# State reads of seven batches with four heads side by side in the TensorE array, transposed by DMA, beside M's session

## The chip, the cores and the metric

The kernel runs on one core of one Trainium2 chip. The metric is the device time of one execution in microseconds; before it is 205.8 us, the median of three runs (205.37 to 205.98). Engines are named as in the profile: PE (TensorE, matrix products into the accumulator memory PSUM), DVE (VectorE), ACT (ScalarE), POOL (GpSimd) and SP (SyncE, which here issues most DMAs). Each engine works through its own instructions in order and meets the others at semaphores.

## What is computed

Cross attention in both directions between 512 rows x and 32 state rows, for 8 batches and 8 heads of 64 columns; then the rows of all heads, side by side, go through a two-layer network with a leaky ReLU.

```
B, H, S, Ns, D = 8, 8, 512, 32, 64          # batches, heads, rows of x, rows of state, columns
a      = softmax(scale * x @ state.T)        # over the state rows
xread  = a @ state
a2     = softmax(scale * state @ x.T)        # over the rows of x
sread  = a2 @ x                              # the read of the states: 32 x 64 for each batch and head
x      = concat([xread, sread], axis=rows)   # heads side by side: (8 * 544) x 512
h      = x @ w_in                            # 512 x 2048
out    = max(0.01 * h, h) @ w_out            # 2048 x 512
```

The change touches `sread = a2 @ x` alone, and the form in which its result is kept.

## The kernel before

The rows that come from x (512 a batch) and those that come from the states (32 a batch) go different ways. For the rows of x the product `xread @ w_in` is not formed from xread: for each batch the kernel computes M = state @ w_in by heads (`a_m`, L326) and then the first layer as a @ M (`ff1`, L347, 16 blocks of 128 output columns each, two matmuls of 512 columns to a block, followed by the leaky ReLU on ACT at L352). The second layer (`Fast.unit`, L532) multiplies in seven products instead of eight on 2 x 2 blocks, with the sums of operands on DVE (L521) and of results on DVE and POOL (L544, L602).

The rows of the states wait until the end. Each batch's read is kept, transposed, in one tile `sr_t` (L141): the 128 partitions are the columns of two neighbouring heads, and the free sizes are 4 pairs of heads and the 256 state rows of all batches. After the last batch, `FastIn` (L365 and on) puts all 256 rows through the first layer, again in seven products: `x_sums` (L398) forms sums of blocks of `sr_t` on DVE, `product` (L416) multiplies weights by blocks of `sr_t` or of those sums.

The order is written by hand: what each engine does comes in the order of the source. The main part is a loop over batches 2 to 7 with 16 steps `s` each. A step has one `ff1` of this batch and some units of the second layer of the batch before (`fill`); between them stand, at fixed steps, the pieces of the next batch's attention: in step 1 its scores (L205) and the last quarter of this batch's M, in steps 5 to 11 its two softmaxes, and behind step 10 the first three quarters of its M. That last group, three blocks of 8 matmuls (24 in all), is called M's session here. The projections of M and the scores run with the array divided in pieces of 64 rows and 32 columns (64*32 in the profile); `ff1` and the second layer use the whole array (128*128).

The read of a state (`a_sread`, L295 to L309) needs `a2T`, the transposed probabilities of the second softmax, which a DMA on SP's queue makes from `a2` (L291); a batch's `a2T` has two buffers. For each pair of heads k it runs 4 matmuls of 64 columns, one for each 128 rows of x; the weights are the 128 columns of both heads of x, the moving operand is the 2 x 32 columns of `a2T` of both heads. Of the four products of two heads by two heads only the two of equal heads are wanted: two ACT casts (L306) take them from PSUM to `sr_t`, 64 partitions each. Batches 0, 1 and 2 are read in steps 4, 6 and 8 of batch 2, and each later batch in its own step 8. The bank is that of tag "big".

PSUM has the tags "ph" (two banks, used in turn by `ff1` and the third block of M's session, which takes both), "py" (two), "big" and "sc" (two banks each as one). A matmul that opens a bank waits until its last reader is done.

On SP's queue stand, in order, loads of x (L99), the transposes of `a2` (L291) and of x (L189), the state loads (L169) with their transposes (L176), and the stores of results (L478, L569). An instruction that waits there holds up those behind it.

Of the kernel before, what the change touches and what calls it, by code (L numbers as in the profile page):

```python
# [9 lines left out]
P = 128  # L10
B, H, S, D = 8, 8, 512, 64
NS = 32
# [3 lines left out]
NT = S // P  # L16
NK = H // 2
SCALE = 1.0 / (D ** 0.5)

BF16 = mybir.dt.bfloat16  # L20
FP32 = mybir.dt.float32
# [6 lines left out]
def kernel(  # L28
# [9 lines left out]
    nc = tc.nc  # L38

    consts = ctx.enter_context(tc.tile_pool(name="consts", bufs=1))  # L40
# [15 lines left out]

    st0f = consts.tile([P, 4, D], FP32, name="st0f")
    nc.scalar.dma_start(  # L60
        st0f[:], state[0:2].rearrange("b h n d -> (b h n) d").rearrange("(p r) d -> p r d", r=4)
    )
# [75 lines left out]
    st1 = consts.tile([P, P], BF16, name="st1")  # L138
    groups = ((2, 4), (4, 8))
    st_t = [consts.tile([P, hi - lo, P], BF16, name=f"st_t{lo}") for lo, hi in groups]  # L140
    sr_t = consts.tile([P, NK, B * NS], BF16, name="sr_t")  # L141

    stb0 = consts.tile([P, 4, D], BF16, name="stb0")

# [14 lines left out]
            ps[:, :, D:].rearrange("p r (k q) -> p k q r", q=8),  # L159
        )  # L160

    stf = [consts.tile([P, hi - lo, P], FP32, name=f"stf{lo}") for lo, hi in groups]
    stb = [consts.tile([P, hi - lo, P], BF16, name=f"stb{lo}") for lo, hi in groups]

    def load_state(i):
# [129 lines left out]
    def a_sread(a):  # L295
        ps = psum.tile([P, NK, 2, NS], FP32, name="psr", tag="big", bufs=1)
        for k in range(NK):
            for i in range(NT):
                nc.tensor.matmul(  # L299
                    ps[:, k, :, :],  # L300
                    lhsT=a.xb[:, i, 2 * k:2 * k + 2, :].rearrange("p h d -> p (h d)"),
                    rhs=a.a2T[:, :, i, NS * k:NS * (k + 1)],
                    start=(i == 0), stop=(i == NT - 1),
                )
        for g in range(2):
            nc.scalar.copy(  # L306
                sr_t[D * g:D * (g + 1), :, NS * a.b:NS * (a.b + 1)],
                ps[D * g:D * (g + 1), :, g, :],
            )  # L309

# [21 lines left out]
    def m_evict(a, c, pm, copy):  # L334
        cols = slice(DM * c, DM * (c + 1))
        if isinstance(pm, list):
            for g in range(2):
                copy(a.M[:, g, cols], pm[g][:])
        else:
            copy(a.M[:, :, cols], pm[:])  # L340
# [24 lines left out]
    class FastIn:  # L365
# [4 lines left out]
        def __init__(self, hT):  # L370
            w = w_in_bf[:].rearrange("p (r k) (i f) -> p i r k f", r=2, i=2)
            self.W = {(i, r): w[:, i - 1, r - 1] for i in (1, 2) for r in (1, 2)}
            x = sr_t[:].rearrange("p (r k) (c t) -> p r c k t", r=2, c=2)
            self.X = {(r, c): x[:, r - 1, c - 1] for r in (1, 2) for c in (1, 2)}
            self.hT, self.S, self.T = hT, {}, {}
            self.bank, self.sv = [{}, {}], [None, None]
# [11 lines left out]
        def x_sums(self):  # L388
            X, T = self.X, self.T
            t = att.tile([P, 4, 2, P], BF16, name="tx", tag="aT")  # L390
            for n in (0, 2, 1, 3):
                u, v, op = (
                    (X[1, 2], X[1, 1], ALU.subtract), (X[1, 1], T.get(2), ALU.subtract),
                    (X[2, 2], X[1, 2], ALU.add), (T.get(1), X[2, 1], ALU.add),
                )[n]
                T[n] = t[:, n]
                with nc.allow_low_precision(reason="operands of a product"):
                    nc.vector.tensor_tensor(out=T[n], in0=u, in1=v, op=op)  # L398

        def product(self, r, n):  # L400
            b = self.bank[r]
            if n in (1, 2):
                tag = ("ph", "ph") if r == 0 else ("big", "sc")
                b[n] = psum.tile([P, self.R, P], FP32, name="pf", tag=tag[n - 1], bufs=2 - r)[:]
            bank = b[n] = b[{1: 1, 6: 1, 7: 1, 4: 1, 2: 2, 5: 2, 3: 2}[n]]
            W, X = self.W, self.X
            lhs = {1: W[1, 1], 2: W[1, 2], 4: W[2, 2]}.get(n)
            if lhs is None:
                lhs = self.S[{3: 3, 5: 0, 6: 1, 7: 2}[n]]
            rhs = {1: X[1, 1], 2: X[2, 1], 3: X[2, 2]}.get(n)  # L410
            if rhs is None:
                rhs = self.T[{4: 3, 5: 0, 6: 1, 7: 2}[n]]
            for q in range(self.R):
                j = self.R * r + q
                for k in range(2):
                    nc.tensor.matmul(  # L416
                        bank[:, q, :], lhsT=lhs[:, k, P * j:P * (j + 1)], rhs=rhs[:, k, :],
                        start=(n in (1, 2, 5) and q == 0 and k == 0), stop=(k == 1),
                        skip_group_check=True,
                    )  # L420
            self.done(r, n, bank)
# [480 lines left out]
    for b in range(2, B):  # L902
        hT = hpool.tile([P, 16, S], BF16, name="hT", tag="hT")
        a = att_of[b]
        nxt = att_of[b + 1] if b + 1 < B else None
        now = Batch(b, hT)
        std = []
        if b == 2:
            std = [(i, 3) for i in range(2)] + [(i, jq) for i in range(2, NT) for jq in range(4)]

        def fill(s):
            n = (PACE2 if b == 2 else PACE)[s]
            left = min(n, len(before.units)) if before else 0
            if left:
                before.run(left)
            if n > left:
                now.run(n - left)

        for s in range(16):
            if s == 11:  # L920
                fill(s)
            ff1(a, hT, s)
            if s == 0:
                if b + 2 < B:
                    load_x(b + 2, nc.sync)
                    open_xb(b + 2)
                a_a2t(a)
                if before:
                    for n in (0, 1):
                        before.f.sums(n, 4, 8)  # L930
            elif s == 1:
                if nxt is not None:
                    a_scores(nxt)
                m_evict(a, 3, a_m(a, 3, "big"), SCA)
                if nxt is not None:
                    a_shift(nxt)
                if b + 2 < B:
                    for h in range(0, H, 2):
                        cast_x(b + 2, h, h + 2, POO)
                if before:  # L940
                    before.f.sums(2, 4, 8)
            elif s == 3:
                if before:
                    before.f.sums(3)
                if nxt is not None:
                    a_max2(nxt)
                if b == 2:
                    weights_sum(0)
                    weights_sum(2)
            elif s == 4:  # L950
                if b == 2:
                    load_state(1)
                    a_sread(a0)
            elif s == 6:
                if b == 2:
                    a_sread(a1)
            elif s == 8:
                a_sread(a)
                if b == 2:
                    state_t(1)  # L960
                    weights_sum(1)
                    weights_sum(3)
            elif s == 12:
                for n in range(3):
                    now.f.sums(n, 0, 4)
            if nxt is None:
                if s == 4:
                    fi = FastIn(None)
                    for n in range(3):
                        fi.w_sum(n)  # L970
                elif s == 10:
                    fi.w_sum(3)
                    fi.x_sums()
            if s == (11 if b == 2 else 7) and b + 2 < B:
                a_open(att_of[b + 2], b + 2)
                a_xt_dma(att_of[b + 2])
            if nxt is not None:
                if s == 5:
                    a_exp(nxt)
                elif s in (7, 8):  # L980
                    a_exp2(nxt, s - 7)
                    if s == 7:
                        a_probs(nxt)
                elif s == 11:
                    a_probs2(nxt)
                elif s in (12, 13):
                    SCA(nxt.M[:, s - 12, DM:2 * DM], pm1[:, s - 12, :])
            if std:
                i, jq = std.pop(0)
                piece(1, h1, i, jq)  # L990
            elif s != 11:
                fill(s)
            if s == 10 and nxt is not None:
                pm0 = a_m(nxt, 0, "big")
                pm1 = a_m(nxt, 1, "sc")
                pm2 = a_m(nxt, 2, "ph")
                for g, copy in enumerate((VEC, SCA)):
                    copy(nxt.M[:, g, 2 * DM:3 * DM], pm2[g][:])
                m_evict(nxt, 0, pm0, SCA)
        before = now  # L1000
# [90 lines left out]
```

## Time and profile before

| | |
|---|---|
| three runs, us | 205.98, 205.37, 205.80 |
| profiled execution, us | 205.83 |
| its span in the profile, us | 204.1 |
| mean granted TensorE clock | 0.997 |
| HBM read / written, MB | 17.30 / 8.91 |

How to read it: times are microseconds from the start of the span unless marked ns. "PE" are matmuls, "PEld" the loads of their weights. Matmuls overlap, and their ends are modelled, so what a matmul costs is read from the distance between the starts of two. A group row names engine, line, operation, output <- inputs, then for PE the part of the array (rows*columns) and the shape (partitions x elements); "xN" is the number of instructions. The chain of waits is followed back from the last instruction to what released each step, and lists pieces with start, length and name. "SPq" is SP's queue, whose rows give the time that the issue of a DMA took.

### The profile page before, as it was taken

To read this page: it belongs to the slowest core of one execution; us is meant where nothing else is said; L and a number is where in the kernel's file an instruction comes from. 1 tells how busy PE (TensorE), PEld (TensorE's weight loads), DVE (VectorE), ACT (ScalarE), POOL (GpSimd) and SP (SyncE) were. 2 spreads that over 40 slices of the span, in tenths; PEclk is the share of its full clock that TensorE was granted. 3 is DMA by queue.
4 is the path that set the end of the run, shared out by engine and by line. 5 is a ranking of instruction groups with operands and counts; after the bars stand their busy time and mean duration, and the time that the engine had idled before them with its cause. 6 is when DMAs were issued, how large, how long until landed. Compare 5 with 4: busy or idle time off the path is not lost.

```text
span 204.1 us, 4531 instructions
## 1 busy us (share of the span) xinstructions
PE 197.5 (97%) x1852; PEld 126.4 (62%) x1852; DVE 152.6 (75%) x231; ACT 145.0 (71%) x272; POOL 40.5 (20%) x66
## 2 busy tenths in 40 slices
PE   7889999999999999999999999999999999999992
PEld 2443534434345557766776767676767677799882
DVE  1767689688999869976996699669968853685622
ACT  3458748579859796978797878788778856467710
POOL 8831002004005104400402040200020002004250
PEclk9999999999999999999999999999999999999998
DMA  6999994889576596939452755250016000410035
GB/s 176 230 207 272 231 248 135 133 273 227 113 230 172 144 171 179 95 114 290 83 95 106 229 131 108 102 157 5 0 53 207 0 3 26 180 55 3 0 90 167
DMA packets 38772, 27.74 MB, mean 136 GB/s; under 512 B 24352, under 2 KB 35744, under 8 KB 38752
## 3 DMA queue, kind: packets, MB, share of 16 engines
q1 hardware_dynamic: 33552, 20.65, 39.6%
q0 software_dynamic: 4912, 6.55, 15.7%
q10 hardware_dynamic: 288, 0.26, 0.6%
q8 instruction: 14, 0.23, 0.4%
q14 instruction: 6, 0.05, 0.1%
HBM read 17.30 MB, written 8.91 MB: 128 GB/s over the span
## 4 chain that ended last, share of the span: by engine, by line
PE 77%; DMA 15%; SPq 2%; POOL 2%; DVE 1%; issue 1%; ACT 1%; POOLq 0%; ACTq 0%
PE yq L532 36%; PE ph L347 22%; DMA x<-in_x_dram 7%; PE py L462 6%; DMA stf<-in_state_dram 3%; PE pf L416 3%; PE yu L532 3%; PE pm L326 3%; DMA xf<-in_x_dram 3%; DMA xT<-xb 2%; PE psr L299 2%; SPq L169 1%; PE sc L205 1%; PE phw L358 1%; ACT M L340 1%
## 5 line engine op out<-in xcount | busy, mean ns | idle before, releaser
L352 ACT ACTIVATE hT<-ph 128x512 bf16<-128x512 f32 x108 | 63.4, 603 | 22.3 <-PE ph L347 21.7
L347 PE MATMUL ph<-aT,M 128*128 128x512 bf16 x216 | 62.3, 379 | 0.0
L532 PEld LDWEIGHTS <-su 128*128 128x128 bf16 x416 | 39.4, 98 | 13.6 <-DVE su L521 1.7
L532 PEld LDWEIGHTS <-hT 128*128 128x128 bf16 x288 | 27.7, 98 | 12.8 <-issue 2.1
L532 PE MATMUL yq<-tw_xf,su 128*128 128x256 bf16 x192 | 27.2, 273 | 0.0
L532 PE MATMUL yq<-w_out_bf,hT 128*128 128x256 bf16 x192 | 27.0, 273 | 0.0
L347 PEld LDWEIGHTS <-M 128*128 128x128 bf16 x216 | 21.0, 98 | 9.4 <-DVE aT L247 0.5
L105 POOL CAST xb<-xl 128x512 bf16<-128x512 f32 (+1 forms) x21 | 14.8, 746 | 57.0 <-DMA xl<-in_x_dram 57.0
L521 DVE TENSOR_TENSOR su<-hT 128x1024 bf16<-128x1024 bf16 x24 | 16.7, 697 | 10.5 <-ACT hT L352 10.5
L462 PE MATMUL py<-w_out_bf,hT 128*128 128x512 bf16 x96 | 24.2, 379 | 0.0
L462 PEld LDWEIGHTS <-hT 128*128 128x128 bf16 x128 | 11.8, 98 | 14.3 <-issue 1.5
L602 POOL TENSOR_TENSOR yo<-sv,sv 128x512 f32<-128x512 f32 x6 | 7.8, 1303 | 57.4 <-ACT sv L541 41.5
L544 DVE TENSOR_TENSOR yo<-yq,sv 128x512 f32<-128x512 f32 x17 | 11.6, 685 | 6.5 <-PE yq L532 6.5
L541 ACT COPY sv<-yq 128x512 f32<-128x512 f32 x24 | 13.9, 585 | 2.0 <-PE yq L532 1.4
L340 ACT CAST M<-pm 128x1024 bf16<-128x1024 f32 x13 | 13.2, 1014 | 0.7 <-PE pm L326 0.6
L532 PE MATMUL yq<-w_out_bf,su 128*128 128x256 bf16 x96 | 13.1, 273 | 0.0
L532 PE MATMUL yq<-tw_x,su 128*128 128x256 bf16 x96 | 13.1, 272 | 0.0
L532 PE MATMUL yq<-tw_x,hT 128*128 128x256 bf16 x88 | 12.1, 273 | 0.0
L273 ACT ACTIVATE e<-sc,mcols 128x512 bf16<-128x512 f32 x16 | 11.0, 692 | 0.1
L215 DVE TRANSPOSE_TENSOR_REDUCE mrow<-sc 128x32 f32<-128x1024 f32 x7 | 8.7, 1244 | 1.5 <-PE sc L205 1.5
L265 DVE TENSOR_REDUCE mcol<-sc 128x2 f32<-128x1024 f32 x8 | 9.7, 1215 | 0.0
L237 DVE TRANSPOSE_TENSOR_REDUCE r<-e 128x32 f32<-128x1024 bf16 x7 | 8.7, 1241 | 0.6 <-ACT e L232 0.6
(145 smaller groups left out, 276.0 us busy)
## 6 DMA issues: line engine op xcount, KB each, us to landing
xl<-in_x_dram SPq DMA_DIRECT2D x5, 1024.0 KB, 6.6
out_dram<-yo SPq DMA_DIRECT2D x10, 512.0 KB, 2.7
w_in_bf<-in_moe_w_in_dram POOLq DMA_DIRECT2D x4, 512.0 KB, 9.1
w_out_bf<-in_moe_w_out_dram POOLq DMA_DIRECT2D x4, 512.0 KB, 16.6
out_dram<-ysb SPq DMA_DIRECT2D x8, 256.0 KB, 4.6
xf<-in_x_dram SPq DMA_DIRECT2D x2, 512.0 KB, 5.0
x<-in_x_dram POOLq DMA_DIRECT2D x2, 512.0 KB, 13.7
xl<-in_x_dram POOLq DMA_DIRECT2D x1, 1024.0 KB, 18.8
```

What stands on the lines that cost most here:

```text
L105: copy(xs[b][:, :, h0:h1].rearrange("p t h d -> p h t d"), xl[b][:, h0:h1].rearrange("p h (t d) -> p h t d", t=NT),)
L215: nc.vector.tensor_reduce(out=m1[:], in_=flat.rearrange("p (c j) -> p c j", j=NS), axis=AX.X, op=ALU.max, apply_transpose=True,)
L265: nc.vector.tensor_reduce(out=m2[:], in_=a.sc[:], axis=AX.X, op=ALU.max, negate=True)
L273: nc.scalar.activation(out=a.e2[:, g], in_=a.sc[:, g, :], func=AF.Exp, bias=a.m2s[:, g:g + 1], scale=SCALE, accum_out=a.r2[:, g:g + 1],)
L340: copy(a.M[:, :, cols], pm[:])
L347: nc.tensor.matmul(ph[:], lhsT=a.M[:, g, P * j:P * (j + 1)], rhs=a.aT[:, g, :], start=(g == 0), stop=(g == 1),)
L352: nc.scalar.activation(out=hT[:, j, :], in_=ph[:], func=AF.Prelu, alpha=0.01)
L462: nc.tensor.matmul(y.py, lhsT=hT[:, j, P * i:P * (i + 1)], rhs=w_out_bf[:, j, :], start=(j == 0), stop=(j == 15),)
L521: (eng or nc.vector).tensor_tensor(out=S[n][:, ms], in0=u[:, ms], in1=v[:, ms], op=op)
L532: nc.tensor.matmul(bank[:, i, :], lhsT=lhs[:, m, P * i:P * (i + 1)], rhs=rhs[:, m, :], start=(first and m == 0 and (i == 0 or of is not No ...
L541: copy(t[:], bank)
L544: nc.vector.tensor_tensor(out=dst, in0=bank, in1=self.sv[n][:], op=ALU.add)
```

## The change

A new function `a_sread_rows` reads the states of one or two batches. For each head pair member g and each 128 rows of x it runs four matmuls, one for each pair k: the weights are the 32 columns of `a2T` of one head, the moving operand the 64 columns of x of that head, and the result goes to 32 partitions of PSUM, so that the four lie in four column quarters of the array (128*32). That is 32 matmuls of 64 columns for a batch. The result is not transposed: rows are state rows of four heads. One ACT copy for each call takes it to a tile `sr_n` in SBUF, of which there is one for batches 0 to 3 and one for batches 4 to 7; they take the place of the tiles `st0f` and `stf2`, which are used only in the beginning. `sread_t` transposes four batches (or three) with one DMA on SP's queue into `sr_t`, whose free sizes are now batch, pair of heads, state row.

The new read takes a bank of tag "ph". Batch 0 is read in step 1 of batch 2 (before: step 4), batches 1 and 2 together ahead of M's session behind step 10 of batch 2 (before: steps 6 and 8), batches 3 to 6 each ahead of M's session behind step 10 of their own loop (before: step 8). The two transposes are issued in step 4 of batch 4 and of batch 7. Batch 7 is still read by `a_sread`, in step 8.

```diff
-    st0f = consts.tile([P, 4, D], FP32, name="st0f")
+    st0f = consts.tile([P, 4, D], FP32, name="st0f", tag="st0f")
...
-    sr_t = consts.tile([P, NK, B * NS], BF16, name="sr_t")
+    sr_t = consts.tile([P, B, NK, NS], BF16, name="sr_t")
+    sr_n = {}
...
-    stf = [consts.tile([P, hi - lo, P], FP32, name=f"stf{lo}") for lo, hi in groups]
+    stf = [consts.tile([P, hi - lo, P], FP32, name=f"stf{lo}", tag=f"stf{lo}") for lo, hi in groups]
...
         for g in range(2):
             nc.scalar.copy(
-                sr_t[D * g:D * (g + 1), :, NS * a.b:NS * (a.b + 1)],
-                ps[D * g:D * (g + 1), :, g, :],
+                sr_t[D * g:D * (g + 1), a.b], ps[D * g:D * (g + 1), :, g, :],
             )
+
+    def a_sread_rows(some):
+
+        ps = psum.tile([P, len(some), 2, D], FP32, name="psn", tag="ph")
+        for u, a in enumerate(some):
+            for g in range(2):
+                for i in range(NT):
+                    for k in range(NK):
+                        nc.tensor.matmul(
+                            ps[NS * k:NS * (k + 1), u, g, :],
+                            lhsT=a.a2T[:, g, i, NS * k:NS * (k + 1)], rhs=a.xb[:, i, 2 * k + g, :],
+                            start=(i == 0), stop=(i == NT - 1),
+                        )
+        c, b0 = divmod(some[0].b, 4)
+        if c not in sr_n:
+            sr_n[c] = consts.tile([P, 4, P], BF16, name=f"sr_n{c}", tag=("st0f", "stf2")[c])
+        nc.scalar.copy(
+            sr_n[c][:, b0:b0 + len(some)], ps[:].rearrange("p u g d -> p u (g d)")
+        )
+
+    def sread_t(c, n):
+        nc.sync.dma_start_transpose(
+            sr_t[:, 4 * c:4 * c + n].rearrange("p b k n -> p b (k n)"),
+            sr_n[c][:, :n].rearrange("p b q -> p (b q)"),
+        )
...
-            x = sr_t[:].rearrange("p (r k) (c t) -> p r c k t", r=2, c=2)
+            x = sr_t[:].rearrange("p (c b) (r k) n -> p r c k b n", r=2, c=2)
...
-                T[n] = t[:, n]
+                T[n] = t[:, n].rearrange("p k (b n) -> p k b n", n=NS)
...
-                        bank[:, q, :], lhsT=lhs[:, k, P * j:P * (j + 1)], rhs=rhs[:, k, :],
+                        bank[:, q, :], lhsT=lhs[:, k, P * j:P * (j + 1)], rhs=rhs[:, k],
...
                 m_evict(a, 3, a_m(a, 3, "big"), SCA)
+                if b == 2:
+                    a_sread_rows([a0])
...
             elif s == 4:
                 if b == 2:
                     load_state(1)
-                    a_sread(a0)
-            elif s == 6:
-                if b == 2:
-                    a_sread(a1)
+                elif b == 4:
+                    sread_t(0, 4)
+                elif b == 7:
+                    sread_t(1, 3)
             elif s == 8:
-                a_sread(a)
+                if nxt is None:
+                    a_sread(a)
...
             if s == 10 and nxt is not None:
+                a_sread_rows([a1, a2] if b == 2 else [a])
                 pm0 = a_m(nxt, 0, "big")
                 pm1 = a_m(nxt, 1, "sc")
                 pm2 = a_m(nxt, 2, "ph")
```

## The prediction

> **What bounds the kernel now.** I read the page first, then the table of four stretches of one batch each, then the waits of TensorE, then the chain of waits around one state read.
>
> ```profile
> span 204.1 us, 4531 instructions
> PE 197.5 (97%) x1852; PEld 126.4 (62%) x1852; DVE 152.6 (75%) x231; ACT 145.0 (71%) x272; POOL 40.5 (20%) x66
> PE yq L532 36%; PE ph L347 22%; DMA x<-in_x_dram 7%; PE py L462 6%; DMA stf<-in_state_dram 3%; PE pf L416 3%; PE yu L532 3%; PE pm L326 3%; DMA xf<-in_x_dram 3%; DMA xT<-xb 2%; PE psr L299 2%; SPq L169 1%; PE sc L205 1%; PE phw L358 1%; ACT M L340 1%
> 75.10:96.20 21.10, 21.10 (x202) 14.77 (x200) 17.55 (x26) 17.02 (x34) 5.01 (x5) 1.00 0.71 165
> 138.50:159.90 21.40, 21.40 (x203) 14.78 (x200) 17.75 (x27) 17.32 (x34) 1.27 (x1) 1.00 0.20 63
> PE phw L358 <- ACT M L340: 0.2, 1, 0.2
> 43.02 1.02 PE phw L358 x4
> ```
>
> In the stretches of batches 3 and 6 (columns: window, sum, then busy time of PE, PEld, DVE, ACT and POOL, granted clock, DMA share, GB/s) TensorE is busy for the whole window at a granted clock of 1.00, while VectorE and ScalarE leave about 4 us of 21 free. Of its waits for another engine that show as idle time, the last is the 0.2 us ahead of L358, near 43 us in the chain. So from 43 us to the end the chain is TensorE itself: a microsecond taken out of its stream comes off the end, unless a new wait eats it. The state read is in that chain:
>
> ```profile
> 84.49 0.43 PE ph L347 x2
> 84.92 0.47 PE psr L299 x16
> 85.39 0.87 PE yq L532 x8
> 58.59 0.63 PE L299 MATMUL psr<-a2T,xb 128*128 128x64 bf16 x16
> 59.05 1.03 PE L462 MATMUL py<-w_out_bf,hT 128*128 128x512 bf16 x4
> 59.28 0.52 ACT L306 CAST sr_t<-psr 64x128 bf16<-64x128 f32 x2
> ```
>
> The first three rows are of the chain (start, length, piece), the others of the timeline. One read is 16 matmuls of 64 columns, from 58.59 to the start of the next matmul at 59.05: 0.46, or 0.029 a matmul; the chain gives 0.47. Nothing is lost on either side of it. The page's 2% for this line is the eight reads, 8 x 0.47 = 3.8 us.
>
> **Removed.** Seven of the eight reads: 7 x 0.467 = 3.27 us of TensorE's stream, and fourteen ScalarE casts of 0.26.
>
> **Added: the matmuls.** A batch now takes 32 matmuls, again 64 columns wide, each with weights of only 32 columns, four of them addressed to four different column quarters of the array. Before has no such matmul 64 columns wide, but has them 128 wide:
>
> ```profile
> 9.05 0.23 PE L670 MATMUL scn<-ident,hi 128*32 128x128 bf16 x4
> 9.11 0.23 PE L670 MATMUL scn<-ident,lo 128*32 128x128 bf16 x4
> 9.44 0.23 PE L670 MATMUL scn<-ident,lo 128*32 128x128 bf16 x4
> 12.28 0.41 PE L670 MATMUL qb<-ident,q 128*32 128x128 bf16 x16 [0.22 <-DVE q L706]
> 12.62 0.41 PE L326 MATMUL pm<-w_in_bf,stbd 64*32 64x512 bf16 x8
> ```
>
> Groups of four follow each other every (9.44 - 9.05)/7 = 0.056, weight loads included, so the four really run side by side: in turn, at 0.029 or more each, a group would need 0.116. Is 0.056 the streaming of 128 columns, or the loading of four weights? If streaming, 64 columns need 0.029 (the pitch of the old read); if loading, it stays 0.056. These are the bounds of one group; below 0.029 nothing in the trace goes at this width. I take 0.029: the old read shows a load of 128 columns finishing behind every 0.029, and a 32-column load is not more than that. With 7 batches x 8 groups = 56 groups this is 1.64 us (3.14 at the upper bound).
>
> The Trainium skill, TensorE: Matmul & The Clock Gate, Part 3, The mechanism, says that a weight load overlaps running matmuls only if it is for another row group; all loads here use all four row groups. Its section LDWEIGHTS gives columns/1.2 ns, so an estimate of 27 ns for 32 columns, and by that rule load and stream would add up to 0.056 a group, the upper bound. The old read's rows speak against it: 16 loads and matmuls on the same row groups in 0.46 us.
>
> **Added: changes of tiling.** The array changes from whole (128*128) or 64*32 to 128*32 and on. M's session (the projections at L326) shows the price on its entry:
>
> ```profile
> 87.83 1.04 PE L532 MATMUL yq<-tw_x,hT 128*128 128x256 bf16 x8
> 88.80 0.84 PE L326 MATMUL pm<-w_in_bf,st_t 64*32 64x512 bf16 x24
> 88.87 0.77 PE pm L326 x24
> L532 PE MATMUL yq<-tw_xf,su 128*128 128x256 bf16 x192 | 27.2, 273 | 0.0
> L670 PE MATMUL qb<-ident,q x32: 219/219/229, 11.7 to 12.5; 128*32 128x128 bf16 x32
> ```
>
> The last L532 matmul (0.273 long) starts at 88.87 - 0.273 = 88.60; M's first comes at 88.80, 0.20 later where 0.109 is the pitch: 0.09 for the change. From 128*32 to 64*32 it is the same: the last L670 matmul (0.219) starts at 12.47, plus 0.056 is 12.53, and M starts at 12.62. Because each new read stands directly beside a 64*32 session, only one change is added for each of the six reads (batch 0 behind L326 in step 1 of batch 2's loop; batches 1 and 2 together, then 3, 4, 5, 6, ahead of M in step 10). 6 x 0.093 = 0.56 us. The first group after a change takes 0.01 more (the sixteen at 12.28 last 0.41, where three pitches, one 0.219 and the 0.01 by which the four of a group are staggered make 0.40): 6 x 0.01 = 0.06.
>
> **Moved: the accumulator.** The read used the bank tag "big", which nothing else wanted between steps 1 and 10. It now takes one of the two "ph" banks, and M's third block (pm2) takes both. So pm2 waits for the new ScalarE copy of the read; behind it in TensorE's order stand the rest of M and everything after.
>
> ```profile
> 69.44 0.59 ACT L998 CAST M<-pm 128x512 bf16<-128x512 f32 x1 [0.79 <-PE pm L326]
> 89.74 0.59 ACT L998 CAST M<-pm 128x512 bf16<-128x512 f32 x1 [1.11 <-PE pm L326]
> L299 PE MATMUL psr<-a2T,xb x128: 192/193/193, 58.6 to 169.5; 128*128 128x64 bf16 x128
> L306 ACT CAST sr_t<-psr x16: 247/259/262, 59.3 to 170.1; 64x128 bf16<-64x128 f32 x16
> L153 ACT CAST stbd<-pst x1: 372/372/372, 4.9 to 4.9; 128x256 bf16<-128x256 f32 x1
> 70.08 1.02 PE L347 MATMUL ph<-aT,M 128*128 128x512 bf16 x4
> ```
>
> ScalarE is idle there (0.79 and 1.11 us ahead of M's copies), so the copy starts at once. Counted from the start R of the read's last group: the matmul ends at R + 0.19, the copy starts 0.06 later (59.22 to 59.28), lasts 0.26 for one batch (same elements per partition as L306's), and the release takes 0.05 (the copy at 69.44 ends at 70.03, TensorE goes on at 70.08): R + 0.56. pm2 is ready at R + 0.029 + 0.093 + two blocks of 0.216 (512 columns, as in the two L347 of 0.43), the first 0.01 longer, = R + 0.56. No wait for one batch, by no margin; for the pair the copy is L153's size, 0.37, so 0.11. I take 0.11 in all; the bounds are 0 and, were a ScalarE operation of 0.6 in front each time, 5 x 0.6 = 3.0. The copy of batch 0 comes behind an L340 copy in step 1 but no bank is wanted from it for two steps (2.6 us). ScalarE on balance does seven copies of 0.26 (two of them as one) in place of fourteen.
>
> **Moved and added on the queue, and the consumers.**
>
> ```profile
> SPq L291 <- PE psr L299: 4.1, 1, 4.1
> L176 SPq DMA_TRANSPOSE st_t<-stb x2: 1197/1234/1272, 35.1 to 67.8; - x2
> DMA to landing us min/median/max: 2.4/2.4/2.4
> 113.42 3.01 SPq L291 DMA_TRANSPOSE a2T<-a  x1
> 121.79 1.87 SPq L189 DMA_TRANSPOSE xT<-xb  x1
> 155.50 1.32 SPq L291 DMA_TRANSPOSE a2T<-a  x1
> 172.30 3.16 SPq L569 DMA_DIRECT2D out_dram<-yo  x2
> 173.32 0.49 DVE L398 TENSOR_TENSOR tx<-sr_t 128x256 bf16<-128x256 bf16 x2
> L416 PE MATMUL pf<-tx,sw x48: 219/219/219, 182.0 to 185.7; 128*128 128x128 bf16 x48
> ```
>
> The two transposes are of L176's size: 1.2 us of issue, 2.4 to land. Both stand on SP's queue right behind an a2T transpose whose issue ends at 116.4 and 156.8, where SP then has nothing until 121.8 and 172.3; the second lands near 160, 13 us ahead of its reader at 173.3. Cost 0; without that cover it would be 1.2 us on an xT that is wanted a batch later. Batch 0's earlier read ends SP's wait of 4.1 us, so batch 2's a2T, two stores and the state loads go out some 4 us sooner; nobody waited for them. L398's operands become runs of 32: if that doubled 4 x 0.29, it would end near 175.6, and its result is first wanted at 182.0. For the L416 matmuls that read sr_t in such runs I take 0: the old read already streams a2T in two runs of 32 at 0.029.
>
> **Sum.** -3.27 + 1.64 + 0.06 + 0.56 + 0.11 = -0.90 us. The profiled execution took 205.83 (span 204.1 and 1.7 around it), which lies 0.03 over the median: 204.93, so 204.9.
>
> **The rivals.**
> A. The weight loads set the pitch. 56 x (0.056 - 0.029) = +1.5: 205.8 + 0.6 = 206.4, slower than before; it decides from a pitch of 0.029 + 0.90/56 = 0.045 on. For it: four loads go in each group, with twice as many loads per streamed column as L670 had. Against it: pitches of 0.216, 0.109, 0.056 and 0.029 for 512, 256, 128 and 64 columns follow the columns alone.
> B. The bank wait. If ScalarE's copy ends late in the five sessions, the whole saving is gone at 0.2 us each; at 0.3 the time is 204.9 + 5 x 0.3 = 206.4. For it: the margin worked out above is nil. Against: ScalarE's idle 0.79 and 1.11.
> C. TensorE gets ahead and waits for the others. The wait behind M in batch 2 (0.14 at 70.08: the six matmuls from 69.28 end their pitch at 69.94) shows how near ScalarE is there. If half of the gain goes this way, 205.3; if all, 205.8. Against it: 4 us of 21 free on both engines.
> D. The four do not run side by side, so the change doesn't do what it says: 7 x 32 x 0.029 = 6.5 in place of 1.64, +4.9: 209.8. The L670 groups speak against it.
> The Trainium skill, TensorEngine Tiling (Array Packing), Instruction Overhead, gives about 60 cycles for each matmul and warns against tiling a dimension that is already small. An estimate from it, 25 ns for each of 32, would make D 208.9; L670's four in 0.056 contradict it, and D keeps a small chance.
>
> **How the numbers follow.** Forecast 0.56, A 0.14, B 0.12, C 0.15, D 0.03. What this kernel's measurement can tell is 0.3%, 0.6 us. The forecast's own range is 204.5 to 205.3 (no bank wait and repeated medians 0.3 apart below; a pitch of 0.035 above), so about 0.52 of its 0.56 is faster; C adds 0.05: 0.57. A lies around +0.6, half of it beyond; B mostly beyond, 0.08; D: slower 0.18. The rest, 0.25, is the same. The range 204.4 to 206.4 takes in A's and B's times and leaves D and the tails of B out.
>
> **What would show it.** Right: groups of four 64-column matmuls every 0.03, a read of 0.24 beside each M session, one change of 0.09 more, no wait at pm2 beyond 0.1, and batches 3 to 6 each about 0.14 shorter. Wrong: a pitch near 0.05 (A); a gap inside M's 24 matmuls ahead of its third block (B); new waits of L347 for ScalarE or VectorE (C); starts 0.03 apart within a group (D); a wait of L398 for the second transpose.

## The result and the profile after

The changed kernel takes 204.87 us (median of six runs, 204.72 to 205.16) beside 205.84 of the kernel before (six runs, 205.37 to 205.98): ratio 0.9955, 95% interval [0.9944, 0.9966]. The profiled execution took 204.74. The change inserts lines, so the new read stands at L318, its ScalarE copy at L326 and the transposing transfers at L331; L326 of before (M) is now L351, L347 (`ff1`) is L372 and L532 (second layer) is L557.

From the page of the changed kernel, the span, the busy times and the chain by line:

```profile
span 202.9 us, 4755 instructions
PE 196.8 (97%) x1964; PEld 125.7 (62%) x1964; DVE 152.7 (75%) x231; ACT 143.3 (71%) x264; POOL 42.3 (21%) x66
PE yq L557 36%; PE ph L372 23%; PE py L487 10%; DMA w_in_bf<-in_moe_w_in_dram 5%; PE pm L351 4%; PE pyw L487 3%; PE pf L441 3%; PE yu L557 3%; PE ph L803 2%; PE psn L318 1%; PE sc L206 1%; PE phw L383 1%; POOL w_in_bf L118 1%; DVE M L365 1%
```

Of TensorE's waits for another engine that stand as idle time the last in time is the one that before had too, near 43 us (columns: us in total, times, longest):

```profile
PE phw L383 <- ACT M L365: 0.2, 1, 0.2
```

TensorE still sets the time: busy 97%, and none of those waits has been added. The read, 2% of the chain before, is 1% (L318, seven batches).

The instructions that touch the read's bank (count, duration min/median/max in ns, first and last start):

```profile
L318 PE MATMUL psn<-xb,a2T x224: 189/193/204, 54.3 to 151.1; 128*32 128x64 bf16 x112
L326 ACT CAST sr_n<-psn x6: 265/267/372, 55.4 to 151.4; 128x128 bf16<-128x128 f32 x5, 128x256 bf16<-128x256 f32 x1
```

And those that touch `sr_t`, with the time to landing of its transfers:

```profile
L331 SPq DMA_TRANSPOSE sr_t<-sr_n x2: 1258/1692/2127, 96.6 to 155.9; - x2
...
L423 DVE TENSOR_TENSOR tx<-sr_t x2: 283/284/285, 172.4 to 172.6; 128x256 bf16<-128x256 bf16 x2
...
DMA to landing us min/median/max: 2.4/3.6/4.9
```

The second transfer is issued at 155.9 and has landed by 161 at the latest; its reader starts at 172.4. That reader takes 0.28 with its operands in runs of 32 elements.

Now the chain of waits of the changed kernel (start, length, piece), the reads and the sessions of M behind them, and under it two rows of the chain of before that the prediction did not show:

```profile
54.37 0.35 PE psn L318 x32
...
67.14 0.63 PE psn L318 x64
67.77 1.01 PE pm L351 x24
...
87.83 0.35 PE psn L318 x32
88.18 0.81 PE pm L351 x24
...
109.23 0.80 PE pm L351 x24
...
151.34 0.81 PE pm L351 x24
```

```profile
110.01 0.77 PE pm L326 x24
...
152.29 0.77 PE pm L326 x24
```

Two things are to be seen. First the read with its change of tiling: 0.35 for one batch, 0.63 for the pair, in place of 0.47 each: 5 x 0.35 + 0.63 = 2.38 in place of 7 x 0.467 = 3.27, a gain of 0.89. Second M's session, 0.77 before in every batch: it is 1.01 behind the pair and 0.80 to 0.81 behind a single read, 0.24 + 0.04 + 0.03 + 0.04 + 0.04 = 0.39 longer. That is the wait of its third block for the bank that the read's copy still holds: by the starts in the trace the first of the block's eight matmuls comes in time, and the second comes 0.05 behind the end of the copy, in all five sessions. It eats nearly half of the gain; e7 and e11 below take it away. Two batches, from 110.01 to 152.29, took 42.28 before; from 109.23 to 151.34 they take 42.11: 0.085 a batch.

How much of the 0.97 between the medians is the change? The first score reduction of the loop and the last matmuls of the program, from the timeline of before and then of the changed kernel:

```profile
41.68 1.25 DVE L215 TRANSPOSE_TENSOR_REDUCE mrow<-sc 128x32 f32<-128x1024 f32 x1 [0.67 <-PE sc L205]
199.37 1.04 PE L532 MATMUL yz<-tw_x,hT 128*128 128x256 bf16 x8
```

```profile
41.30 1.25 DVE L216 TRANSPOSE_TENSOR_REDUCE mrow<-sc 128x32 f32<-128x1024 f32 x1 [0.57 <-PE sc L206]
198.66 0.82 PE L557 MATMUL yz<-tw_x,hT 128*128 128x256 bf16 x6
```

The last matmul (0.273 long) starts at 199.37 + 1.04 - 0.273 = 200.14 before and at 198.66 + 0.82 - 0.273 = 199.21 after. So the stretch from the score reduction of batch 2 to the last matmul, in which everything that was changed lies, went from 158.45 to 157.91: 0.54. I call it the stretch below. The 0.38 by which the reduction itself comes earlier can't be put down to the change: over all profiled kernels of this study, none of which changes what runs ahead of it, that point lies between 41.2 and 42.4 without any order, and the changed kernel itself, profiled again, has it at 42.36. From the start of the last matmul to the end of the span it is 3.92 before and 3.74 after.

### The profile page after: what moved, and what is told of

Its sections match the earlier page's. It is cut to its first block, busy times and chain, and to the rows that moved or that the text cites. A ratio compares the mean times of both kernels' runs of the same rounds, so it can differ in the third digit from the quotient of the medians.

```text
span 202.9 us, 4755 instructions
## 1 busy us (share of the span) xinstructions
PE 196.8 (97%) x1964; PEld 125.7 (62%) x1964; DVE 152.7 (75%) x231; ACT 143.3 (71%) x264; POOL 42.3 (21%) x66
## 4 chain that ended last, share of the span: by engine, by line
PE 89%; DMA 5%; POOL 2%; ACT 1%; DVE 1%; issue 0%; POOLq 0%
PE yq L557 36%; PE ph L372 23%; PE py L487 10%; DMA w_in_bf<-in_moe_w_in_dram 5%; PE pm L351 4%; PE pyw L487 3%; PE pf L441 3%; PE yu L557 3%; PE ph L803 2%; PE psn L318 1%; PE sc L206 1%; PE phw L383 1%; POOL w_in_bf L118 1%; DVE M L365 1%; ACT hT L377 1%; ACT M L365 1%
## 5 line engine op out<-in xcount | busy, mean ns | idle before, releaser
L372 PE MATMUL ph<-aT,M 128*128 128x512 bf16 x216 | 62.3, 379 | 0.0
L557 PEld LDWEIGHTS <-su 128*128 128x128 bf16 x416 | 39.7, 98 | 14.5 <-DVE su L546 1.7
L557 PEld LDWEIGHTS <-hT 128*128 128x128 bf16 x288 | 27.7, 98 | 11.8 <-issue 1.1
L105 POOL CAST xb<-xl 128x512 bf16<-128x512 f32 (+1 forms) x21 | 16.4, 818 | 61.1 <-DMA xl<-in_x_dram 61.1
L557 PE MATMUL yq<-tw_xf,su 128*128 128x256 bf16 x192 | 27.2, 273 | 0.0
L557 PE MATMUL yq<-w_out_bf,hT 128*128 128x256 bf16 x192 | 27.0, 273 | 0.0
L372 PEld LDWEIGHTS <-M 128*128 128x128 bf16 x216 | 21.0, 98 | 9.1 <-DVE r L280 0.4
L557 PE MATMUL yq<-w_out_bf,su 128*128 128x256 bf16 x96 | 13.1, 273 | 0.0
L557 PE MATMUL yq<-tw_x,su 128*128 128x256 bf16 x96 | 13.1, 273 | 0.0
L557 PE MATMUL yq<-tw_x,hT 128*128 128x256 bf16 x88 | 12.1, 273 | 0.0
L224 DVE STREAM_TRANSPOSE mrowb<-mrow 128x1024 f32<-128x1024 f32 x7 | 8.7, 1245 | 0.2
```

What stands on the lines that cost most here:

```text
L105: copy(xs[b][:, :, h0:h1].rearrange("p t h d -> p h t d"), xl[b][:, h0:h1].rearrange("p h (t d) -> p h t d", t=NT),)
L372: nc.tensor.matmul(ph[:], lhsT=a.M[:, g, P * j:P * (j + 1)], rhs=a.aT[:, g, :], start=(g == 0), stop=(g == 1),)
L557: nc.tensor.matmul(bank[:, i, :], lhsT=lhs[:, m, P * i:P * (i + 1)], rhs=rhs[:, m, :], start=(first and m == 0 and (i == 0 or of is not No ...
```

## The experiments

The diffs are against the changed kernel where nothing else is said. Three groups were each run beside the kernel before: e1 to e4 (its median 205.70 in 23 runs), e5 to e8 (205.94 in 14), e9 to e11 (205.73 in 12).

**Is the new layout of sr_t free?** The layout and the views of the consumers alone, with all eight reads as before:

```diff
-                if b == 2:
-                    a_sread_rows([a0])
...
-                elif b == 4:
-                    sread_t(0, 4)
-                elif b == 7:
-                    sread_t(1, 3)
+                    a_sread(a0)
+            elif s == 6:
+                if b == 2:
+                    a_sread(a1)
             elif s == 8:
-                if nxt is None:
-                    a_sread(a)
+                a_sread(a)
...
-                a_sread_rows([a1, a2] if b == 2 else [a])
```

> Only the new layout of sr_t (batch, pair of heads, state row), the tags of the two tiles and the readers' views; all eight reads are the old ones in their old steps. Theory (the whole gain comes from TensorE's stream in the reads): no change, 205.8 us, within 0.2. Rival (the 0.4 us by which the profiled after was already ahead at 42 us, and the 0.2 behind its last matmul, come with the layout): 205.2 to 205.4. A loss here would mean that the readers' runs of 32 columns cost: 48 matmuls at up to 0.056 more, 208.5 at most.

Measured: 205.70, ratio 1.000 [0.9989, 1.0011], stretch 158.45, the same as before to the hundredth. The consumers cost nothing.

**Does it matter where the read stands?** The new reads in the old steps, in the old bank:

```diff
-        ps = psum.tile([P, len(some), 2, D], FP32, name="psn", tag="ph")
+        ps = psum.tile([P, len(some), 2, D], FP32, name="psn", tag="big", bufs=1)
...
-                if b == 2:
-                    a_sread_rows([a0])
...
                     load_state(1)
+                    a_sread_rows([a0])
...
+            elif s == 6:
+                if b == 2:
+                    a_sread_rows([a1])
...
                 if nxt is None:
                     a_sread(a)
+                else:
+                    a_sread_rows([a])
...
-                a_sread_rows([a1, a2] if b == 2 else [a])
```

> The new reads in the old steps 4, 6 and 8, in the old bank, so away from M's session: each of the seven pays two changes of tiling, and none waits at pm2. By the after trace one read then costs 0.094 (change in) + 0.223 + 0.029 + 0.097 (change out) = 0.443 us against 0.466 of the old one: 7 x -0.023 = -0.16, 205.7 us. Rival (the place is of no account, the narrow matmuls alone give the gain): 204.5 to 204.9. Rival (there is a gain of 0.4 outside the reads that comes with the change): 205.3.

Measured: 205.77, ratio 0.9999 [0.999, 1.0008], stretch 158.36. The chain shows M's session undisturbed:

```profile
88.33 0.77 PE pm L351 x24
...
109.45 0.77 PE pm L351 x24
```

A batch takes 21.12 here and 21.14 before (from 88.87 to 110.01). Four heads side by side are worth next to nothing where both changes of tiling have to be paid; the gain comes from standing beside a 64*32 session, as the sum had it.

**What sets the pitch?** Each read's matmuls issued twice:

```diff
-        for u, a in enumerate(some):
+        for u, a in list(enumerate(some)) * 2:
```

> Each new read's matmuls run twice into the same bank (the result is the same), so every session doubles. By the forecast's pitch of 0.029 a group: 56 x 0.029 = 1.64 us more, 206.5. By the after trace, where the double session of batches 1 and 2 fell from 0.029 to about 0.034 a group after its tenth group: five sessions of 16 groups with 6 at 0.034, and one of 32, 1.84 more, 206.7, and the longer session shows the slower pitch from about its tenth group in every batch. By rival A (loads set the pitch, 0.056): 3.1 more, 208.0.

Measured: 207.87, ratio 1.0114 [1.0101, 1.0127], 1.2 more than the theory's 206.7. The chain and the timeline of this kernel at the read of the pair, now 128 matmuls:

```profile
67.95 1.18 PE psn L318 x128
...
69.68 0.79 issue
...
90.06 0.62 PE psn L318 x64
```

```profile
67.88 1.25 PE L318 MATMUL psn<-xb,a2T 128*32 128x64 bf16 x128
...
69.21 0.37 ACT L326 CAST sr_n<-psn 128x256 bf16<-128x256 f32 x1 [1.19 <-PE psn L318]
...
70.47 0.59 PE L351 MATMUL pm<-w_in_bf,st_t 64*32 64x512 bf16 x9 [0.79 <-issue]
```

The starts in the trace tell it apart: the first ten groups of a session follow each other every 0.029, the later ones every 0.033, that is one load and matmul each 0.0083. 128 matmuls take 1.06 from first to last start; at a pitch of 0.056 (rival A) they would take 31 x 0.056 = 1.74. So A falls, and the later pitch is a limit of its own, 14% above the streaming. Most of the missing time is the 0.79 in both fences: M's last nine matmuls wait for nothing that the profile shows. The bank is not it: the read's copy ends at 69.58 (69.21 + 0.37), and the nine are one more than the third block, which alone needs the bank. That TensorE had run out of instructions there is the likeliest reading, but it is not shown; a transfer of 16 KB on the instruction queue (q8) runs from 67.76 to 68.88 in this trace, and what waited for it the trace doesn't tell. The standstill happens once, behind the longest session, and not in the changed kernel. With it the stretch, 160.66 and so 2.75 over the changed kernel's 157.91, is about accounted for: 5 x (0.62 - 0.35) + (1.18 - 0.63) + 0.79 = 2.69.

**Do the four run side by side because of their order?** One pair k after the other, so that consecutive matmuls stay in one column quarter:

```diff
-            for g in range(2):
-                for i in range(NT):
-                    for k in range(NK):
+            for k in range(NK):
+                for g in range(2):
+                    for i in range(NT):
```

> The same 32 matmuls of a read with the pair of heads as the outer loop, so that eight in a row go to the same column quarter. Theory (it is the four neighbours in four quarters that run together): each takes its 0.029 in turn, 32 x 0.029 = 0.93 in place of 0.235 a batch, 7 x 0.70 = 4.9 us more than after, 209.8. Rival (the array sorts them out of its queue, the order is of no account): 204.9. If a load of 32 columns took longer than the stream of 64, it would come out above 209.8.

Measured: 207.48, ratio 1.0089 [1.0074, 1.0103], between the two. The timeline at batch 3's read, and the chain at the pair's read and at batch 3's:

```profile
89.12 0.80 PE L318 MATMUL psn<-xb,a2T 128*32 128x64 bf16 x32
```

```profile
68.02 1.26 PE psn L318 x64
...
89.19 0.73 PE psn L318 x32
89.92 0.77 PE pm L351 x24
```

32 matmuls take 0.80 - 0.193 = 0.61 from first to last start, 0.0196 each, where 0.029 each would be 0.90 and four at a time 0.22. A matmul's record doesn't name its quarter, but one reading fits all 32 starts: the eight of a quarter are 0.029 apart (0.038 behind the first), and the next quarter's first comes 0.006 behind the fifth of the one before, so that two quarters overlap for a while. So the order does matter, by 5 x (0.73 - 0.35) + (1.26 - 0.63) = 2.5 of reads. Against that stand shorter waits at M, whose session behind a single read is back at 0.77; the stretch is 160.18, 2.3 longer than the changed kernel's. The Trainium skill, TensorEngine Tiling (Array Packing), Instruction Overhead, has about 60 cycles for each matmul, 0.025 us by the prediction's estimate; 0.0196 and, side by side, 0.0073 for each (0.029 / 4) do not bear that out as a cost of the single instruction.

**The changed kernel again**, unaltered:

> The changed kernel once more, for a closer interval. From the batch-2 score reduction on VectorE to the last matmul its trace is 0.54 us shorter than that of before, while ahead of it the profiled executions of all kernels so far lie up to 0.9 us apart without a pattern. Theory (only the reads count, the beginning is chance): 0.54 us faster than before, and the six runs of 0.97 were partly luck: 205.1 to 205.3. Rival (there is a gain outside the reads too): 204.7 to 204.9.

Measured: 205.12, ratio 0.9961 [0.9947, 0.9976], stretch 157.82: 0.63 shorter than before. In this execution's chain M's session behind the pair is shorter:

```profile
68.83 0.92 PE pm L351 x24
```

With the 1.01 of the first the pair's wait is thus 0.15 to 0.24 over the 0.77.

**Do the transposes on the queue cost anything?** Both issued twice:

```diff
                 elif b == 4:
                     sread_t(0, 4)
+                    sread_t(0, 4)
                 elif b == 7:
                     sread_t(1, 3)
+                    sread_t(1, 3)
```

> Each of the two transposes of the reads is issued twice. Theory (they stand where SP's queue has nothing to do and their readers come much later): no difference from the changed kernel, within 0.2 us. Rival (each issue of 1.3 to 2.1 us delays an xT or a store that is wanted): up to 2 us slower.

Measured: 205.03, ratio 0.9957 [0.9943, 0.9971], stretch 157.80. Nothing: the queue's cover holds even for double.

**Is the missing gain the wait for the bank?** The reads moved behind the last quarter of M in step 1 of the next batch, also beside a 64*32 session, where no block of M asks for a "ph" bank:

```diff
-                if b == 2:
-                    a_sread_rows([a0])
+                a_sread_rows([a0] if b == 2 else [a1, a2] if b == 3 else [att_of[b - 1]])
...
-                    a_sread_rows([a1, a2] if b == 2 else [a])
```

> The reads ahead of M's session move behind the M block in step 1 of the next batch, where batch 0's read is already: batches 1 and 2 in batch 3's step 1, batches 3 to 6 in the next one's. As many changes of tiling as in the changed kernel, but M's third block no longer waits for the copy of the read. The after trace has that wait at 0.03 in four sessions and 0.24 in the double one, so 0.37 us faster than the changed kernel run with it. Rival (the wait hides behind other work, or ScalarE, which has a 1.0 us cast in that step, passes it on): no gain, or slower. Rival (the forecast's 0.11 for all of it): 0.1 faster.

Measured: 205.19, ratio 0.9967 [0.9953, 0.998], stretch 158.04: no gain. Yet M's session is back at 0.77, in this kernel's chain:

```profile
68.45 6.40 DMA xT<-xb
...
88.44 0.77 PE pm L351 x24
```

The first row is what took the place. TensorE's waits name it, and the timeline shows it on the queue:

```profile
PE sc L206 <- DMA xT<-xb: 0.4, 1, 0.4
```

```profile
66.57 1.20 SPq L177 DMA_TRANSPOSE st_t<-stb  x1
67.86 0.53 SPq L503 DMA_DIRECT2D out_dram<-ysb  x1
68.45 2.24 SPq L190 DMA_TRANSPOSE xT<-xb  x1
...
74.89 0.41 PE L206 MATMUL sc<-xT,st_t 64*32 64x512 bf16 x8 [0.42 <-DMA xT<-xb]
```

Batch 4's x transpose stands behind a state's transpose and a store, takes until 74.85 from the start of its issue at 68.45, and the scores of batch 4 wait for it. They are ready earlier here because the pair's read, which stood ahead of them, now stands behind them. Counted from batch 2's score reduction they start at 33.62 in the changed kernel (74.92 - 41.30), and at 32.76 in e11 below, where they wait for nothing (74.46 - 41.70): 0.86 sooner, the read's 0.63 and the 0.24 of the wait behind it; xT lands at 33.21 here (74.85 - 41.64). In the changed kernel's timeline the same scores have no wait behind them:

```profile
68.11 3.97 SPq L190 DMA_TRANSPOSE xT<-xb  x1
...
74.92 0.41 PE L206 MATMUL sc<-xT,st_t 64*32 64x512 bf16 x8
```

**Two reads at a time**, to save changes of tiling as well: batch 0 alone, then 1 and 2, 3 and 4, 5 and 6, each in step 1. Batches 3 and 4 belong to two tiles `sr_n`, so their read is taken over by two ScalarE copies.

```diff
+                if b in (2, 3, 5, 7):
+                    a_sread_rows({2: [a0], 3: [a1, a2], 5: att_of[3:5], 7: att_of[5:7]}[b])
...
-                elif b == 4:
+                elif b == 5:
                     sread_t(0, 4)
```

> As e7_step1, but read in pairs: batch 0, then 1 and 2, 3 and 4, 5 and 6, in step 1 of batches 2, 3, 5 and 7: four sessions in place of six. Two changes of 0.093 and two slow first groups of 0.01 fewer, 0.21; given back by the slower pitch behind the tenth group of a double session, 0.04 each in two more: 0.13 us faster than e7_step1. Rival (a double session runs the instruction supply dry, as the session of 128 matmuls in e3_twice did): slower by up to 0.8 each.

Measured: 205.08, ratio 0.9959 [0.9945, 0.9974], stretch 157.93, with the same wait for xT (0.4 in the list of waits). That is 0.11 of stretch less than e7, where 0.13 was expected, and none of the three sessions of 64 matmuls is followed by a standstill as in e3.

**That transfer moved ahead.** Three kernels with one more edit: e9 is e8 with it, e10 the changed kernel with it, e11 e7 with it.

```diff
-            if s == (11 if b == 2 else 7) and b + 2 < B:
+            if s == 7 and b + 2 < B:
                 a_open(att_of[b + 2], b + 2)
                 a_xt_dma(att_of[b + 2])
```

> The kernel of e8_pairs, with one transfer moved: the transpose that makes batch 4's xT is issued in step 7 of batch 2 in place of step 11, ahead of the store and of the state's transfer that stood before it on SP's queue. Theory (the reads' net gain is eaten by the wait of M's third block for the bank of psn, 0.28 to 0.37 us in all, and in e7_step1 and e8_pairs the 0.49 us that the scores of batch 4 wait for xT took what the removal of that wait gave): xT lands about 4 us earlier, the scores no longer wait, and the stretch from the score reduction of batch 2 to the last matmul shortens from 157.93 to about 157.4; ratio to the kernel before about 0.9937 (204.5 us beside 205.8). Rival (another transfer or engine is late at that place next): the 0.49 comes back under another name, ratio 0.996.

> The changed kernel with that one transfer moved and nothing else. Theory: in the changed kernel the scores of batch 4 do not wait for xT (it lands 0.8 us before them), so the move by itself gives nothing: ratio 0.996, stretch 157.8 to 157.9. Rival (the xT transfer holds a part of the gain back in the changed kernel too): ratio 0.994 and a stretch of about 157.4.

> The kernel of e7_step1 (each read behind the M block of step 1, the pair in one bank) with that one transfer moved. Theory: the wait for the bank of psn is gone as in e7_step1, the scores of batch 4 no longer wait, so about 0.37 us less than the changed kernel: stretch about 157.5, ratio about 0.994. Rival: as for e9_pairs_xt7, ratio 0.996.

| | median, us | ratio to before | stretch, us | expected stretch |
|---|---|---|---|---|
| e9, pairs | 204.36 | 0.9933 [0.9918, 0.9948] | 157.44 | 157.4 |
| e10, changed kernel | 204.90 | 0.9963 [0.9948, 0.9978] | 157.93 | 157.8 to 157.9 |
| e11, step 1 | 204.77 | 0.9950 [0.9936, 0.9964] | 157.56 | 157.5 |

All three stretches came out within 0.06 of the theory. In e9 the queue's and TensorE's rows at the place, and the chain:

```profile
64.55 1.89 SPq L190 DMA_TRANSPOSE xT<-xb  x1
...
74.40 0.41 PE L206 MATMUL sc<-xT,st_t 64*32 64x512 bf16 x8
```

```profile
75.02 0.63 PE psn L318 x64
...
87.94 0.77 PE pm L356 x24
...
158.77 0.63 PE psn L318 x64
```

The transfer is issued 3.9 earlier than in e7, the scores wait for nothing (no bracket), and M's session is 0.77. e11 against e10, which differ in the place of the reads alone, gives the price of the bank wait: 157.93 - 157.56 = 0.37 of stretch. e9 is the fastest kernel of the study: 1.37 under the kernel before, and 0.54 under the changed kernel with the same transfer moved.

## Why the prediction was right, and where its sum was not

The forecast was 204.9 with a sum of -0.90 against the profiled 205.83; the median is 204.87. The direction and its cause are as forecast, but the sum and the result agree more closely than the terms do, and that is luck. With the chain's pieces for the reads and the wait the sum is -3.27 + 2.38 + 0.39 = -0.50, and the stretch moved by 0.54: 0.4 of the forecast gain isn't there, 0.28 of it at the wait and 0.12 at the reads. The repeat and the kernel with only xT's transfer moved (e10, which that move leaves as it is) put the gain at 0.82 and 0.83 (205.94 - 205.12, 205.73 - 204.90). Of that the stretch gives 0.52 to 0.63, and 0.18 lies between the last matmul and the end of the span, which no step of the sum had. What the first 0.97 has beyond that is no more than the start varies by.

The 0.18 at the end comes with the two added transfers, not with the reads. From the start of the last matmul to the end it is 3.92 and 3.89 in the kernels without them (before and e1), 3.73 to 3.75 in the ten with two, and 3.62 in e6 with four. At the end SP goes through nine waits for semaphores in a fixed order, 0.06 apart where nothing holds them up. The last one that is held up, 2.65 to 2.71 behind the start of the last matmul, has five behind it in before and e1, three in the kernels with two more transfers on SP's queue, and one in e6: two steps fewer are 0.12 of the 0.18, and the held-up wait itself ends 0.04 to 0.05 sooner with the added transfers. The medians can't tell a part as small as this: by it e2 should be 0.27 faster than before, and its median is 0.07 slower.

- **Removed, 3.27:** right. In e9 and e11 the stretch follows from the chain's pieces alone: 158.45 - 3.27 + 0.35 + 3 x 0.63 = 157.42 (measured 157.44), and 158.45 - 3.27 + 5 x 0.35 + 0.63 = 157.56 (157.56).
- **The pitch, 0.029:** right for single reads, though one took 0.35 in place of the sum's 0.335 (8 x 0.029 + 0.01 + 0.093), which leaves out the 0.01 by which the last group's four are staggered. From the eleventh group of a session on the pitch is 0.033, so the pair took 0.63 in place of the 0.57 of the sum (16 x 0.029 + 0.01 + 0.093). The rule that the prediction took from the Trainium skill, TensorE: Matmul & The Clock Gate, Part 3, The mechanism, that loads overlap running matmuls only if they are for another row group, is not borne out: 32 such loads and matmuls in 0.35, change of tiling included. The same section also has a load into the background weight buffer pulled ahead of running matmuls, which would fit; no trace here shows that buffer.
- **The changes of tiling, 6 x 0.093, and where the read must stand:** right. e2 pays one more for each read and gains 0.09 of stretch.
- **The wait at pm2, 0.11:** the step that failed. "No wait for one batch, by no margin" was 0.04 each, and the pair's 0.11 was 0.15 to 0.24, over the 0.1 that the prediction itself had named as the bound: 0.29 to 0.39 by the chain's rows, 0.37 by e11 against e10. The timeline of the changed kernel shows how the margin went, and the last two rows, of the repeat, the pair there:

```profile
67.07 0.70 PE L318 MATMUL psn<-xb,a2T 128*32 128x64 bf16 x64
...
67.95 0.37 ACT L326 CAST sr_n<-psn 128x256 bf16<-128x256 f32 x1 [0.74 <-PE psn L318]
68.38 0.10 PEld L351 LDWEIGHTS <-st_t 64*32 64x32 bf16 x6 [0.35 <-issue]
...
87.76 0.42 PE L318 MATMUL psn<-xb,a2T 128*32 128x64 bf16 x32
88.11 0.88 PE L351 MATMUL pm<-w_in_bf,st_t 64*32 64x512 bf16 x24
88.26 0.27 ACT L326 CAST sr_n<-psn 128x128 bf16<-128x128 f32 x1 [0.67 <-PE psn L318]
```

```profile
68.13 0.70 PE L318 MATMUL psn<-xb,a2T 128*32 128x64 bf16 x64
...
68.92 0.37 ACT L326 CAST sr_n<-psn 128x256 bf16<-128x256 f32 x1 [0.64 <-PE psn L318]
```

  For batch 3 the last read matmul starts at 87.76 + 0.42 - 0.193 = 87.99 (R, here 0.01 behind the start of its group, from which the prediction counted). M starts at R + 0.12, as forecast; the copy starts at R + 0.27, not 0.25, and takes 0.27, not 0.26. For the pair R is 67.58, the copy starts at R + 0.37, and the weights of the last six matmuls of M's third block are loaded only at 68.38, 0.06 behind the copy's end. A margin worked out as nil was no cover: what the terms were off by, 0.03, became a wait of 0.03 to 0.04, four times over. Rival B is thus true in kind at a quarter of its size (0.07 a session on the mean, not 0.3). In the repeat the pair's copy starts at R + 0.28 (R = 68.13 + 0.70 - 0.193 = 68.64); why it came 0.1 later in the first execution stays open.
- **Batches 3 to 6 about 0.14 shorter:** 0.085, the read's 0.12 (0.47 - 0.35) less the 0.04 of the wait.
- **Queue and consumers, 0:** right for the loop and for what reads `sr_t` (e1, e6). That the added transfers shorten the end was not seen.
- **Rival C** did not come in the changed kernel: no new wait of TensorE for ScalarE or VectorE stands in its list. What came in e7 and e8 is of another kind, a wait for a transfer, and came from moving the pair's read behind the scores of batch 4. The prediction looked along SP's queue for what the moved transfers hold up; it did not ask which transfer has the least slack. In the changed kernel xT lands 0.84 ahead of those scores (74.08 and 74.92), in the kernel before 0.39 (75.10 and 75.49).
- **Rival D** fell with the groups of four, and e4 shows that even in turn it would have cost 2.3 us of stretch over the changed kernel, not 4.9.

Left open are the pair's later copy in the first execution and the standstill in e3.

## What to carry to other kernels

When a price is found to be hidden "by no margin", put the uncertainty of its terms into the sum for each time it occurs, or give the accumulator a bank that nothing asks for next. Dividing the array in column quarters paid for small products here only where a divided session already stood beside them, since the two changes of tiling cost nearly what the packing gives. And moving work from ahead of a consumer to behind it brings that consumer forward by the whole work, not only by the gain: look for the transfer with the least slack ahead of it, and move that one up in its queue along with the change.

## What the runs showed of the hardware that was not expected

- In the sessions of 64 and 128, short matmuls with a weight load each come every 0.0083 us once some 40 of them have passed; up to there they come every 0.0073 (0.029 for four).
- Behind 128 such pairs and fifteen of M's matmuls TensorE stood still for 0.79 us for nothing that the profile shows (e3, one execution profiled); behind 64 it did not.
- With heads in turn the starts fit 0.029 within a column quarter, with the next quarter beginning 0.006 behind the fifth of eight, 0.0196 on the mean (e4).
- Two more transfers on SP's queue, issued long before, made the end of the program 0.18 us shorter, by their place among SP's last waits (before and e1 beside the others).
- The start of the steady loop differs by up to 1.2 us between profiled executions of kernels that do the same up to there (41.2 to 42.4), more than the whole effect; 1.06 of it between two executions of the changed kernel (41.30 and 42.36). A stretch between two marks inside the loop told kernels 0.1 apart where the spans did not.
